# A new table of order, engines and buffers for four layers of two kinds of linear attention

## The chip, the core and the metric

The kernel runs on one core of one Trainium2 chip. The metric is device time in microseconds (us); the median of three runs is quoted, and single executions are named where a profile is read. Below, TensorE (PE; PEld is its weight load), VectorE (DVE), ScalarE (ACT), GpSimd (POOL) and SyncE (SP) are the core's engines. Each runs its own queue of instructions strictly in order and waits on semaphores for the others. Operands lie in SBUF; TensorE writes its results to PSUM.

## What is computed

x is 2048 tokens of 512 numbers (bf16). Four layers are added to it, A, B, A, B, each on a normalised x:

```python
x = A_x
x = x + _A_ref(_layernorm(x), A_wq, A_wk, A_wv, A_wo, A_beta)
x = x + _B_ref(_layernorm(x), B_wqkv, B_w_phi, B_wo)
x = x + _A_ref(_layernorm(x), ...)
x = x + _B_ref(_layernorm(x), ...)
```

Both have 32 heads of 16 numbers. Layer A cuts the tokens into 4 segments of 512. Within a segment it is causal softmax attention; from one segment to the next a memory is carried and read with phi(t) = t + 1 for positive t, else exp(t):

```python
p = softmax(q_s k_s^T * scale + mask);  a_dot = p @ v_s
a_mem = (phi(q_s) @ M) / (phi(q_s) @ z + 1e-6)
o = g * a_mem + (1 - g) * a_dot;  M += phi(k_s)^T v_s;  z += sum(phi(k_s))
```

Layer B has no mask: with a 16 x 16 map w_phi per head and phi(t) = [softmax(t w_phi), softmax(-t w_phi)],

```python
kv = phi_k^T v;  z = sum(phi_k);  o = (phi_q @ kv) / (phi_q @ z + 1e-6);  return o @ wo
```

## The kernel before

The tokens are 16 tiles of 128; x stays in SBUF as X. All the work is first written down as a graph of 2904 operations (class `Graph`, function `op`): each names its engine or engines, what it reads and writes, and the buffers that it opens. An operation is one instruction on ScalarE, VectorE and GpSimd, one or two transfers on SyncE, and 1 to 32 matmuls on TensorE, each with a weight load of its own: 1165 operations, 12,085 matmuls.

What the graph holds, layer by layer (`build`):

- `ln` normalises a tile: statistics on VectorE (L599, L600), the inverse root on GpSimd (L607, L609), the scaling on VectorE (L620), and a transpose, by a transfer of SyncE (L364) or on TensorE (L380, emptied through L359 or L360).
- `a_proj` projects queries, keys and values of a segment of layer A (L341), masks the keys into four copies (VectorE, L686, or ScalarE, L688), applies phi (L351, L674, L675) and sends the values through DRAM (v_rows, L368) to put them in rows.
- `a_att` computes the scores of two tiles (label S and, along the diagonal, Sd; TensorE, L326, D<-pK,pQ), takes their exponential out of PSUM (ScalarE, L351, 256 x 128x1024 and 192 along the diagonal), and multiplies with the values (label PV; L326, D<-pW,p and D<-pW,pP). A reciprocal (L393) and a product (L906) on VectorE empty the result.
- `b_keys` and `b_query` do the same for layer B: exponentials on ScalarE, sums on VectorE (L1012, L1015), small matmuls with the memory (label Zq: D<-Rz,p; label N: D<-Rkv,p; both L326), and products on VectorE (L1117, L1123).
- `out_proj` projects the result (L341) and adds it to X (VectorE, L961); in the last layer it stores X.
- `setup` loads the weights and x and fills small constants: lines 507 to 561 are such writes, among them the memsets of L553, L556 and L561, which are needed only when the buffer that they fill is first used, and the cast of L514, whose result nothing reads.

PSUM is four tensors D0 to D3 of 128x1024 f32. Every result of TensorE takes one of them from its first matmul to its last reading; 603 tiles share the four in turn, so TensorE often waits for a buffer to be emptied by ScalarE or VectorE. SBUF buffers are shared in the same way (pools p1, p2, pS and so on).

The order is not worked out in the kernel. `place` reads it from `ORDER`, a packed string at the end of the file. Unpacked, it has three parts: the operations' numbers in the order in which they are to stand (two bytes each), the engine of each operation (one byte), and the buffer of each of 1479 tiles (one byte). An engine's queue is the table's order cut down to that engine's operations. A tile that takes a buffer waits for the last operations on the tile that had it before. `emit` then writes the five queues and puts in the waits; a wait that another one already covers is left out.

```python
order = [self.ops[i] for i in np.frombuffer(raw, "<u2", n)]
o.seq, o.eng = k, ENGS[raw[2 * n + o.id]]
slots = dict(zip(tiles, raw[3 * n:]))
```

Of the kernel before, what the change touches and what calls it, by code (L numbers as in the profile page):

```python
# [16 lines left out]
D = 512  # L17
H = 32
# [42 lines left out]
class Tile:  # L61
# [236 lines left out]
class Kernel:  # L298
# [908 lines left out]
c-q~01C%YvvUWtIvs$OSk8RtwZQHhO+qP}nwr$&fRlCpJnYnk?y!+O_-oMs;xqDYuRz^lfeDOu>tkrRVL1IV_0QI0g5Hx^>&<LVIV`u_Rp&2xXWDp(VLOiGjnV~wAhxkweBxHk<Py<Rq  # L1207
R%ih&p%o~o3AvyGRD^<12y#MeXal987PN&jPzl;W3@8f;pfD7H_Rs-pLs38|1~H*Bl!M~X5n@3d=mec1AtZwAkOQhfUFZ!dAr)BY0=Xdxe1{+K6RN^%2!uD_Krr-yx6l_1e1z067}CHX
0PG3_;3**Xhj-8qy1@__3Q6G^aOe&LAvfm1_wWfm!xtC@d9erdgo%(3d%-l!iNhcl22lp^1H$z%12@2Q3`c`dz)YMA&*23O#t9GvmOemn%m}&IJa`GOU?Y^kuP_|Oz$WO2{V|wAXex|`
qF4+^!Z%m~4n=}3Fb#&_e8|E!!*&<}L(z}6LP?wsJ760`qX9SvRzWHBCx**lCuD)yFbQYEK->iyRs+XbFc||eEzE!^7=%k9I*o<Xum;NGR1|1&5|qUPxEzXLK`e|FFdXK`wJ;3JVLm8>  # L1210
XQ4E%gF?6hD&k5Qj`MH?#-K_V4#vTJ91j675+}oc9EDThFzkl|cmy1bKnLI;B*f7eKt~}MBhnr?2{CCe&cWTV4`*Q_j75>i4`<^7*b9j<KkS1EI0iGpSk$O+F)YO;I2RjW6I_gouo^bR
g_sVSVpLd()$u$mz{6-TB}OKRXJ8fXqKP;T7r}Tez?R{1Jc3nlH>JWxSQ%?z3P_Dru`$NRwOA9Qz(qJf>o5vkfJ+buS5bXT$7*41tcwew9yZ5=6c^LOYKo76R0mt&IoOOXu^G0)E!Y}Q
;wjvSo6sMUV0es&$MFQV!M1n^{4oTh(sc->qZoh@@CNLm^SA@EvIH0rFW@oUircXr?xo|f4WnZkTtk=P3be<A7!5-)Hm#-b)B$(nYCMN~Fa{ojLwFX~;Ck$cJ@5>6!VTD(R$wGNjXg0L
uArTmo@HQdXcxxBmb8*mP-pCd4e26Y!pIm4yJCGxj@>XNMa5Rsi1twpN<}HK0bRzV7>D*#FYJwduqL&o+EkZnQ9FuDQLqjbWc6qX#iQJ;J6?q=cnvyJV!A;$X(@G~tGJ0aQv$k%*YPek
rzX^xhEgXQM$M=%wx=6-6K`P%+<|-8fjUwP8crjqDRrf5^cd4(H@c74X(Yv`6EKRN-~-HxPcb9Dz=!w@vtcGIK$-C+X2;&thk8;kDoCeb5GAB#G=Y{=dc2K~Fas8%@$?+W&^Q`MqbVJB
r~cHJ22ej*M`I}om7pWEo`%q1I!YVp4i=`8l!x7djg*Z|q)C*Wm7-&GoDNYA)`Jey7D`H~X&X(Zt@Ie4KoR<ciRc}D#*8d4drx0*I~8Kz@fGI4T=W+2P(GHM^3V@FOH=48zM<E+gU--h
+DRv<Fnde)=p@~z+famEp=30bp3!M4%F@s&x=P>h9G$02G>x9qbh=Ep=n%`qa<bc$kKW@0I?O&%F?vK<@Dlq>KauDuy}`@uF{Put^om~72TV^#*hf6d($YivK}G2+eW3jGg)&eFmYIE|
($tY9r@`zA{iGpmAmfyuU1NjT3lcPsGSWM|&fM}vFX;xGPYdWKW7L&(W8dfkNy-b~Nzp~hN(WeR%0$4BX<A6xs4O#dkPT%g*f3U(on&RHCmYE|u@P(r^<v#wZ$@l58^g-89;_l8&B{|5
%1*b~ZN}IDR)J2jiqwboW96tX%L6&75@n%dtUo)=j<cCGi)Pb4wx1PaIcO}q!ZK5FHjZ6ol6PWfSP7>1ImX#Nc8AR&!S1tCtTL5klD%R6>>+!=?y^Pnmd$04*hMyvy<&4IfZc>D^q9S7
# [80 lines left out]
```

## Time and profile before

| | us |
|---|---|
| median of 3 runs | 456.07 |
| the runs | 455.7, 462.07, 456.07 |
| the profiled execution | 456.51 |
| its span, first to last instruction | 454.8 |

A row of groups gives line, engine, operation, what it writes and reads, the number, then busy time, mean time of one in ns, and the idle time of the engine just before them with what ended it. A row of waits gives who waited for what, the total in us, how many times, and the longest. A row of windows gives the stretch, then the busy time of PE, PEld, DVE, ACT and POOL with the number of instructions, the granted clock, the share of the transfer engines and GB/s. A row of the time line gives start and length in us and, in brackets, the idle time before. "issue" stands where an engine waited for nothing that the profile names. Queue q8 carries instructions: the transfers that bring TensorE's program to its sequencer. TensorE's busy time is modelled at the ends of matmuls, so it overstates.

### The profile page before, as it was taken

To read this page: it belongs to the slowest core of one execution; us is meant where nothing else is said; L and a number is where in the kernel's file an instruction comes from. 1 tells how busy PE (TensorE), PEld (TensorE's weight loads), DVE (VectorE), ACT (ScalarE), POOL (GpSimd) and SP (SyncE) were. 2 spreads that over 40 slices of the span, in tenths; PEclk is the share of its full clock that TensorE was granted. 3 is DMA by queue.
4 is the path that set the end of the run, shared out by engine and by line. 5 is a ranking of instruction groups with operands and counts; after the bars stand their busy time and mean duration, and the time that the engine had idled before them with its cause. 6 is when DMAs were issued, how large, how long until landed. Compare 5 with 4: busy or idle time off the path is not lost.

```text
span 454.8 us, 26184 instructions
## 1 busy us (share of the span) xinstructions
PE 427.2 (94%) x12085; PEld 289.5 (64%) x12085; DVE 403.1 (89%) x766; ACT 420.9 (93%) x584; POOL 58.4 (13%) x146
## 2 busy tenths in 40 slices
PE   8999999999999989989999998999999988999787
PEld 4756667767766666655556666677677666765444
DVE  7999999998798978869999997999898896788897
ACT  5999999999999997899999999999899999699992
POOL 3411014010101101100330112020020020110000
PEclk9999999999999999999999999999999999999999
DMA  8976655564247212101255668436232414300355
GB/s 251 217 165 100 99 93 109 107 87 80 45 76 111 38 40 50 13 3 27 62 111 86 85 97 103 71 87 81 57 50 49 109 19 63 46 17 4 49 91 180
DMA packets 105167, 36.71 MB, mean 81 GB/s; under 512 B 91730, under 2 KB 105058, under 8 KB 105058
## 3 DMA queue, kind: packets, MB, share of 16 engines
q1 hardware_dynamic: 104226, 34.50, 42.9%
q8 instruction: 95, 1.56, 1.4%
q10 hardware_dynamic: 800, 0.52, 0.4%
q14 instruction: 14, 0.11, 0.1%
q0 software_dynamic: 32, 0.02, 0.0%
HBM read 10.76 MB, written 6.55 MB: 38 GB/s over the span
## 4 chain that ended last, share of the span: by engine, by line
PE 61%; ACT 20%; DVE 12%; issue 3%; DMA 3%; POOL 1%; DVEq 0%
PE D L341 38%; PE D L326 22%; ACT p L351 11%; ACT pP L351 7%; DVE X L961 2%; DVE pQ L686 1%; DVE p L1117 1%; DVE stats L599 1%; DMA pX<-p 1%; DMA p<-p 1%; ACT pS L351 1%; DVE p L620 1%; DMA X<-in_A_x_dram 1%; DVE pK L360 1%; DVE p L906 1%
## 5 line engine op out<-in xcount | busy, mean ns | idle before, releaser
L351 ACT ACTIVATE p<-D 128x1024 bf16<-128x1024 f32 (+1 forms) x256 | 225.6, 934 | 10.8 <-PE D L341 4.9
L351 ACT ACTIVATE pP<-D 128x640 bf16<-128x640 f32 (+2 forms) x192 | 149.5, 828 | 7.2 <-PE D L326 5.9
L326 PE MATMUL D<-pK,pQ 64*128 64x128 bf16 (+6 forms) x1792 | 112.0, 227 | 4.2 <-ACT p L351 1.0
L326 PEld LDWEIGHTS D<-pK,pQ 64*128 64x128 bf16 x1792 | 67.0, 93 | 40.2 <-ACT pP L351 8.5
L326 PE MATMUL D<-pW,pP 64*128 64x50 bf16 (+1 forms) x3072 | 84.0, 181 | 3.4 <-issue 2.7
L326 PEld LDWEIGHTS D<-pW,pP 64*128 64x128 bf16 x3072 | 68.6, 93 | 9.2 <-issue 3.8
L607 POOL TENSOR_SCALAR rstd<-mv 128x1 f32<-128x1 f32 x60 | 17.0, 288 | 340.8 <-DVE mv L600 340.4
L326 PE MATMUL D<-pW,p 64*128 64x50 bf16 (+1 forms) x2048 | 50.4, 181 | 0.4 <-DVE pQ L686 0.2
L326 PEld LDWEIGHTS D<-pW,p 64*128 64x128 bf16 x2048 | 44.3, 93 | 3.9 <-issue 1.1
L599 DVE BATCH_NORM_STATS2 stats<-X 128x6 f32<-128x512 bf16 x63 | 42.3, 679 | 1.9 <-DMA X<-in_A_x_dram 1.6
L961 DVE TENSOR_TENSOR X<-X,D 128x1024 bf16<-128x1024 bf16 (+1 forms) x36 | 39.2, 1096 | 5.1 <-PE D L341 4.6
L326 PE MATMUL D<-tri,rep 64*128 64x64 bf16 (+1 forms) x384 | 40.1, 197 | 0.0
L341 PE MATMUL D<-pX,WA_k 64*128 64x512 bf16 (+1 forms) x288 | 37.4, 353 | 1.0 <-issue 0.5
L341 PE MATMUL D<-pX,WA_q 64*128 64x512 bf16 (+1 forms) x288 | 37.7, 353 | 0.6 <-issue 0.6
L609 POOL TENSOR_TENSOR rstd<-rstd,mhalf 128x1 f32<-128x1 f32 x60 | 35.9, 604 | 3.4
L341 PE MATMUL D<-WB_k,pX 64*128 64x512 bf16 (+1 forms) x288 | 33.8, 352 | 1.1 <-DMA pX<-p 0.4
L341 PE MATMUL D<-WA_o,p 64*128 64x512 bf16 (+1 forms) x288 | 33.2, 352 | 1.6 <-issue 0.8
L1015 DVE TENSOR_REDUCE pS<-p 128x64 f32<-128x1024 bf16 x28 | 33.4, 1211 | 0.9 <-ACT p L351 0.9
L341 PE MATMUL D<-WB_v,pX 64*128 64x512 bf16 (+1 forms) x288 | 33.3, 352 | 0.0
L341 PE MATMUL D<-WA_v,pX 64*128 64x512 bf16 x256 | 33.2, 377 | 0.0
L341 PE MATMUL D<-WB_o,p 64*128 64x512 bf16 (+1 forms) x288 | 32.5, 353 | 0.4 <-ACT p L351 0.3
L341 PE MATMUL D<-pX,WB_q 64*128 64x512 bf16 x256 | 32.5, 376 | 0.3 <-ACT p L351 0.3
(123 smaller groups left out, 665.5 us busy)
## 6 DMA issues: line engine op xcount, KB each, us to landing
v_rows<-pV SPq DMA_DIRECT2D x16, 272.0 KB, 3.6
pW<-v_rows SPq DMA_DIRECT2D x64, 68.0 KB, 2.7
out_dram<-X SPq DMA_DIRECT2D x7, 256.0 KB, 2.6
X<-in_A_x_dram SPq DMA_DIRECT2D x3, 512.0 KB, 7.7
pX<-in_B_wqkv_dram SPq DMA_DIRECT2D x3, 512.0 KB, 4.5
p<-p SPq DMA_TRANSPOSE x73, 3.2
pX<-p SPq DMA_TRANSPOSE x54, 3.6
WA_k<-in_A_wk_dram SPq DMA_DIRECT2D x2, 256.0 KB, 7.2
```

The source lines that it names most:

```text
L326: ins = e.matmul(out_ap, lhsT, rhs, start=st, stop=sp, tile_position=(basep(lhsT), basep(out_ap)))
L341: ins = e.matmul(out_ap, lhsT[64 * hf:64 * hf + 64], rhs[64 * hf:64 * hf + 64], start=k == 0 and i == 0, stop=k == 1 and i == len(lists[hf ...
L351: return self.g.op({"act": (dur, lambda e: e.activation(out_ap(), in_ap(), func, scale=scale))}, reads, writes, opens, label=label)
L360: "dve": ((340 if fast else n / 0.96 + 65), lambda e: e.tensor_copy(out_ap(), in_ap()))}
L599: v(lambda e: e.bn_stats(self.stats[:, t, :], self.X[:, t, :]), 602, [R("X", t)], [R("st", t)], label="bn")
L607: v(lambda e: e.tensor_scalar(rs, self.mv[:, t, 1:2], LN_EPS, None, op0=ALU.add), 170, [R("mv", t)], [R("rstd", t)], eng="pool", label="rstd")
L609: v(lambda e: e.tensor_tensor(rs, rs, self.mhalf[:], ALU.pow), 540, [R("rstd", t), R("mhalf")], [R("rstd", t)], eng="pool", label="rstd")
L620: v(lambda e: e.tensor_scalar(xn.t[:], self.X[:, t, :], self.mv[:, t, 0:1], self.rstd[:, t:t + 1], op0=ALU.subtract, op1=ALU.mult), 300, [ ...
L686: ch = {"dve": (129 + n / 3.84, lambda e, sl=sl, out=out: e.tensor_scalar(out(), src(), self.m4[:, sl:sl + 1], None, op0=ALU.mult))}
L906: v(lambda e, pvv=pvv, rden=rden, part=part: e.tensor_tensor(part(o).rearrange("p (a h d) -> p a h d", a=2, h=16), pvv()[:, :, :, 0:16], r ...
L961: self.v(lambda e: e.tensor_tensor(X(), X(), src(), ALU.add), 65 + 512 * n / 0.96, pr + xr, xr, label="res")
L1015: v(lambda e, E=E, k=k, Z=Z: e.tensor_reduce(Z.t[:, 64 * k:64 * k + 64], E.t[:].rearrange("p (a f h) -> p a h f", a=16, h=4), AX.X, ALU.ad ...
```

## The change

Only the string `ORDER` is replaced. The operations, their instructions and their sizes are the same; the code that reads the table is the same. The table was found by an offline search over orders in which the transfers that bring TensorE's instructions were taken to arrive later than for the table before. Start and end of each string:

```diff
 ORDER = """
-c-q~01C%YvvUWtIvs$OSk8RtwZQHhO+qP}nwr$&fRlCpJnYnk?y!+O_-oMs;xqDYuRz^lfeDOu>tkrRVL1IV_0QI0g5Hx^>&<LVIV`u_Rp&2xXWDp(VLOiGjnV~wAhxkweBxHk<Py<Rq
...
-a?d|MpPY5jE1bv!T{3!=EP%Up1cK4em6nW$c%gGK@l(v0K!jk9!J7QgVGtmg^v7_a9-zSn1HAu{_<<W(H^a0-KewD&Qsj#a(*&-F?+oE6j~}R!{tKc#=CJ
+c-q~11C%YvvUWy9x=y=~ZQHhO+qP}nwr$(CZQFiTyU*O2xp&sQ`_{kSzt(-VyQ?ZIBLiQ25j(3_6JsnntH<iI2CN}V%;K=PEFO!`kY#3#SYuX=HDOIzGiF(NR)R%i$yiBNodK)CO0niF
...
+>}$i4^zh@M;Bp`sDbyvC8=iK3aCN%Nh3|bzYnKb5f(0lqL4Lw==C}xlkO}hsToK^*7FQ2yLw<_Fx#m&3#V1JxdQ1r>x99o#n)eTIZkcem?2!HoOSk5$
 """
```

Unpacked, the two tables differ as follows (places are counted in each engine's own queue).

| engine | operations before, after | in the same place | furthest move |
|---|---|---|---|
| TensorE | 1165, 1165 | 664 | 16 places |
| ScalarE | 583, 582 | 494 | 4 |
| VectorE | 766, 769 | 107 | 62 |
| SyncE | 248, 248 | 97 | 22 |
| GpSimd | 142, 140 | 14 | 25 |

Five operations change engine: three memsets of setup go from GpSimd to VectorE (one of L556, two of L561), one of L561 goes the other way, and one emptying of a transposed tile in the last stage goes from ScalarE (L359) to VectorE (L360). Of 1479 tiles, 1034 have another buffer number; in PSUM, 431 of 603 have another number, and 462 of 603 follow the same tile in their buffer as before.

At the start, SyncE's queue has the load of X's tiles 4 to 7 ahead of the first half of WA_k, and the loads of WA_v and of one part of WA_o ahead of those of X's tiles 8 to 15. In VectorE's queue, statistics and masks stand at other places among the emptyings of PSUM. In the last stage one of the two last tiles' products (L1117) stands behind an addition to X (L961), and the cast of L514 stands just ahead of it.

More of the change, by code (lines that the diff above doesn't have):

```diff
@@ L1211 @@
[L1211 to L1218, printed above, removed]
@@ L1259 @@
[L1259 to L1261 removed]
+c-q~11C%YvvUWy9x=y=~ZQHhO+qP}nwr$(CZQFiTyU*O2xp&sQ`_{kSzt(-VyQ?ZIBLiQ25j(3_6JsnntH<iI2CN}V%;K=PEFO!`kY#3#SYuX=HDOIzGiF(NR)R%i$yiBNodK)CO0niF
@@ new lines @@
+D{H}8vYIR>tH83c9IPU1#agq1tPm^BYOzc#J1fH^E6j?pHmogc$11VftSoEKin4?(7wf=^F~#bz%B&pg$U3nqtT?O7s<LpbGkeN<vy?0mOT}`tF6=u?!uqfu>?eE8`m)q41B=dLu$b%(
+OT!Ff5Q}|egIH2Fm<?cESvQuE4PpIR0tWDm^<%-TI~&N}vUe;ud}5zj4>pwbWC1KM^kVN>P8h{F%LDl!7ddPid||l&VLcnpW<VfrV1f-}(;*0-vzagm=CX-wFa)v*tT@bL7GJQJEDQU<
+HnL!R#j;Qd*u+BcE9(bSSyAW@qggQ+!@jW*Yzf=S=Cf&R2ux?&*)moVX0jb@8ygC%*Z`Qrwy+tj6hy<F%)yatHQUSxX0xociw%UcY!WPGYuGHtAppj*$uI>1K|on30F&5MNXyDVdB_jT
+SrAyL07YOeD+tkX7z~Hfu#Odma<GCGf_bo#jbrm65*q;(p%RRQ{V<sYvGMFM3x@~54@bcimYepoJ!~{AVn^6+76A{igb)MwvZKs_m>3K9F$D)%Fzkg{un!W!9GDGbU;@mAlPn@G0Rv+p
@@ new lines @@
+KT8aYnS`a#0GhxeSPa!59B60=E1@Y=hXS+!4#PrN1t}pCMn=t|;4Yj9<DfE}X6e{?IKz&>0=5j6!*2A)D&WUbL276OHJ~cQhQ@H7t%dZgCLF+ZaFLy3Nnjzn#NxmztOK>6C4}NZtP3ev
+eOQgHARX0)%@Bocfw<5b{Gc8*gXVC71z-zk1L^4`Y=l$b4{c!+gok)=9Imsd7y|L(1hj*r5CLwmW8lv&z#iO-+aUo&gsrd*cEE8K9oFD^xXjwa6?PCJK`2CnwU`WI;~wY$hhR0tfOBvb
+cEfsD105keMrCK<7;B9yum|*n4UmUU!%pY~X<!#zgru+nT4Ec_Kq+t~rhrRuh&9CI5E)`YXNU^*u@$DoRM-gjVK3+nm!Sscr3Tmq`am3v0{gKh_Jy`s8|z{%Y=?1i33i1#SP!qVY!nZ#
+KsUI?I^zvoiixo?CcvxE1vg<6yasonDK^J@a1)2(X6%H`@H*Up4tNuWVS5~oEwCeY#cmkFu3>k03?uM5W`L0x6Gq_^$O=#41;oeu@Bkh{M##&uL0ZTTncxn41_kgXJc3)$8~b2-$P7L4
@@ L1262 @@
+D;rjPK0^AVXT_^l(g6a4T<K62#$@suM4;P}yzb+Q5Hlf;$13UX>&@gAUKsz#*LxU*YOngjg7tWfhPypOpr30dB+M1BZnZn~6`V^G@)JP8Zdlw`Kg?sV0e=eevEHjpw<R&~3-AC9=3YoT
+>}$i4^zh@M;Bp`sDbyvC8=iK3aCN%Nh3|bzYnKb5f(0lqL4Lw==C}xlkO}hsToK^*7FQ2yLw<_Fx#m&3#V1JxdQ1r>x99o#n)eTIZkcem?2!HoOSk5$
 """
```

90 lines of the change are left out of this document (44 added, 46 removed).

## The prediction

> **What bounds the kernel now.** I read the page first, then the waits, then the time line at the longest waits, then counts between them.
>
> ```profile
> span 454.8 us, 26184 instructions
> PE 427.2 (94%) x12085; PEld 289.5 (64%) x12085; DVE 403.1 (89%) x766; ACT 420.9 (93%) x584; POOL 58.4 (13%) x146
> ...
> q8 instruction: 95, 1.56, 1.4%
> ...
> PE 61%; ACT 20%; DVE 12%; issue 3%; DMA 3%; POOL 1%; DVEq 0%
> ...
> L351 ACT ACTIVATE p<-D 128x1024 bf16<-128x1024 f32 (+1 forms) x256 | 225.6, 934 | 10.8 <-PE D L341 4.9
> L351 ACT ACTIVATE pP<-D 128x640 bf16<-128x640 f32 (+2 forms) x192 | 149.5, 828 | 7.2 <-PE D L326 5.9
> ```
>
> The profiled execution took 456.51 us around a span of 454.8, so 1.7 lie outside; the median of the runs shown is 456.07, 0.4 below it, and I carry sums over to the median. TensorE, ScalarE and VectorE are busy 94, 93 and 89% of one span: there is no single engine to relieve. Two ScalarE groups that empty PSUM alone hold 225.6 + 149.5 = 375 us. The windows show where the idle time lies.
>
> ```profile
> 0.00:5.00 5.00, 3.89 (x24) 1.48 (x26) 1.94 (x5) 1.85 (x3) 3.17 (x20) 1.00 0.60 180
> 5.00:440.00 435.00, 412.53 (x11873) 282.21 (x11869) 389.74 (x747) 412.37 (x573) 55.19 (x126) 1.00 0.44 77
> 440.00:455.00 15.00, 10.74 (x198) 5.78 (x192) 11.45 (x16) 6.64 (x11) 0.00 (x0) 0.99 0.53 152
> ```
>
> Between 5 and 440 us ScalarE works 412.37 of 435 and TensorE 412.53: 22.5 us are free on each, and 2% of the time (9.1 us) would be two fifths of that. The clock is 1.00 throughout, so it explains nothing here. What ends those idle times:
>
> ```profile
> PEld D L326 <- ACT pP L351: 10.4, 34, 1.1
> PEld D L326 <- ACT p L351: 9.7, 29, 0.8
> ...
> DVE pS L393 <- PE D L326: 8.3, 10, 1.7
> ...
> PE D L326 <- issue: 4.9, 7, 1.6
> ...
> PE D L341 <- issue: 2.5, 5, 0.8
> ```
>
> Weight loads wait for ScalarE to empty a PSUM buffer (63 times), and matmuls wait for "issue", nothing the profile names, 12 times, 4.9 + 2.5 = 7.4 us. I looked at the longest of these, and at the instruction transfers just before it (a window of 422.3 to 423.6).
>
> ```profile
> 422.71 0.40 PEld L326 LDWEIGHTS D<-Rz,p 64*128 64x128 bf16 x26
> ...
> 424.77 0.24 PE L326 MATMUL D<-Rz,p 64*128 64x48 bf16 x7 [1.55 <-issue]
> q8 instruction: 1, 0.02, 4.5%
> ```
>
> TensorE stops within an operation of identical matmuls and goes on 1.55 us later; the only packet that window holds is one 16 KB packet of queue q8. There are 95 such packets, so 24,170 / 95 = 254 TensorE instructions each. If these waits are for that transfer, they must lie whole packets apart. Windows from one such wait to the next:
>
> ```profile
> 145.96:166.51 20.55, 18.29 (x637) 13.38 (x637) 17.38 (x26) 19.53 (x28) 1.92 (x4) 1.00 0.25 46
> 281.11:323.54 42.44, 41.71 (x1273) 28.96 (x1274) 38.75 (x65) 40.27 (x55) 5.13 (x13) 1.00 0.48 80
> 374.06:424.76 50.70, 46.43 (x1274) 33.77 (x1275) 39.52 (x77) 44.52 (x67) 3.22 (x8) 1.00 0.20 29
> ```
>
> Matmuls plus weight loads are 1274, 2547 and 2549: 5, 10 and 10 packets of 254.8. So the "issue" waits are TensorE's own instructions arriving late, where a packet's worth of short matmuls runs faster than the next one comes.
>
> The Trainium skill, "Runtime: NRT & Kernel Launch", section "Instruction fetch mechanics", gives the block as 16 KiB, 256 instructions, and here the trace agrees; it also says the fetch is hidden because instructions are dispatched more slowly than blocks arrive. By that, no gain from this source exists and the rival that lives on it (below) falls away; the 7.4 us above contradict it, so I keep that rival.
>
> **The change part by part.** Decoding both tables gives the same 2904 operations. TensorE: 664 of 1165 in the same place of its queue, none moved by over 16 places; of the swapped pairs within 24 places about two thirds are PV against PV, another fifth PV against a score matmul. ScalarE: 494 of 583 unmoved, none by over 4. VectorE: 107 of 766 unmoved, up to 62 places; SyncE 97 of 248, up to 22; GpSimd 14 of 142. Five operations change engine. No duration changes; the price is only in who waits.
>
> *Instruction packets.* Cut at every 254.4 TensorE instructions, the new queue holds in each packet on average 18 instructions that the old one did not; of the 12 packets that ended in a wait, ten differ by 64 or fewer, two by 107. Relieving a wait would need a packet with clearly longer matmuls. I take 0; the ends are -7.4 (all waits gone) and +1.55 (one more of the longest).
>
> *VectorE's order.* It empties 208 readings of PSUM. Adding the traced durations of what is queued ahead of each in both orders, the work ahead grows by 0.08 us on average; 38 have over 0.4 more (90th percentile 0.66), 31 over 0.4 less, 4 over 1 more.
>
> ```profile
> L686 DVE TENSOR_SCALAR pQ<-p,m 128x1024 bf16<-128x1024 bf16 (+1 forms) x70 | 31.1, 457 | 0.0
> ...
> L360 DVE CAST WB_q<-D 128x512 bf16<-128x512 f32 x4 | 2.8, 690 | 1.0 <-PE D L326 1.0
> L556 POOL MEMSET pP<- x6: 197/308/411, 1.5 to 3.6; 128x128 bf16 x2, 128x384 bf16 x2, 128x256 bf16 x2
> L561 DVE MEMSET pT<- x1: 112/112/112, 39.2 to 39.2; 128x64 bf16 x1
> L514 DVE CAST H8b<-H x1: 155/155/155, 418.6 to 418.6; 128x8 bf16<-128x8 f32 x1
> ```
>
> What changes places there is typically one mask (0.457 us) or a normalisation against a reading, and a shift in one reading is mostly made up by the next, as the mean of 0.08 shows. I take 0; the ends are -12 (31 x 0.4 all on the path) and +25 (38 x 0.66 all on the path). They are bounds, not expectations: the shifts have both signs, and each engine is idle only a twentieth of the time, so most land on covered work.
>
> *PSUM buffers.* Of 603 tiles in the four buffers, 462 still follow the same tile as before in their buffer; the others follow from the swaps in TensorE's queue, since a buffer is handed on in the order of use. ScalarE empties in an order that differs in 89 places of 583, each by at most four. That the 63 waits on ScalarE above (10.4 + 9.7 = 20.1 us) change is possible in both directions; I take 0, with a quarter of them, 5 us, either way.
>
> *Head.* A memset of line 556 goes from GpSimd to VectorE, just ahead of the first normalisation, and one addition of line 521 behind it goes later. The load of X's tiles 4 to 7 (512 KB) is issued ahead of the first half of WA_k (256 KB) instead of behind; the last two lines are the landings of WA_k and of X.
>
> ```profile
> 6.92 0.41 DVE L620 TENSOR_SCALAR p<-X,mv,rstd 128x512 bf16<-128x512 bf16 x1
> ...
> 7.24 0.22 DVE L521 TENSOR_TENSOR rep<-rep,ident 128x128 bf16<-128x128 bf16 x1
> ...
> 7.38 0.17 PEld L380 LDWEIGHTS D<-ident,p 64*128 64x128 bf16 x8 [0.97 <-DVE p L620]
> ...
> 9.21 0.09 PEld L341 LDWEIGHTS D<-pX,WA_k 64*128 64x128 bf16 x1
> 1.93 0.40 SPq L462 DMA_DIRECT2D WA_k<-in_A_wk_dram  x1
> DMA to landing us min/median/max: 5.3/5.3/5.3
> DMA to landing us min/median/max: 6.3/6.3/6.3
> ```
>
> The memset costs 0.31, the addition gives back 0.22: +0.1 on the way to the first projection (ends 0 and +0.41, its slowest). WA_k landed at 1.93 + 5.3 = 7.2; X, issued at 2.4 with 6.3 to landing, at 8.7. Swapped, both are in by about 8.7, and the projection starts at 9.21: 0 (end: +0.5, if WA_k takes 1 us behind X).
>
> *Transfers behind SyncE.* 65 loads, stores and transposes shift by over 2.5 us in SyncE's queue. Two transposes stand in the chain of work:
>
> ```profile
> 66.28 4.52 DMA pX<-p
> 354.79 4.13 DMA p<-p
> 70.89 0.39 PE L341 MATMUL D<-WB_k,pX 64*128 64x512 bf16 x2 [0.41 <-DMA pX<-p]
> 61.48 0.40 DVE L620 TENSOR_SCALAR p<-X,mv,rstd 128x512 bf16<-128x512 bf16 x1
> 63.58 0.41 DVE L620 TENSOR_SCALAR p<-X,mv,rstd 128x512 bf16<-128x512 bf16 x1
> ```
>
> At 66 us the projection of B's keys needs both tiles of a pair. Their normalisations ended at 61.9 and 64.0, yet the second transpose went out only at 66.28, behind other transfers. The new VectorE order puts the first tile's normalisation behind the second's and behind one long multiply (L835), about 65.8 to 66.2, and SyncE's new order has the other tile's transpose and one load ahead of it, both gone by then: it goes out at about 66.3, lands at 70.8 as before, and TensorE waits its 0.41 again. At 354.79 the ten VectorE operations between the emptying of a key projection and the reciprocal that leads to the transpose are the same ten in another order. I take 0 for both; the ends are -0.4 (that wait gone) and +4.5, one transpose fully uncovered.
>
> *Setup writes.* One 0.11 memset goes onto VectorE at the last query stage (419 us), where TensorE waits for VectorE, and the unused 0.155 cast of line 514 leaves that place: 0.
>
> *Tail.* One emptying of a transposed tile (0.60 on ScalarE) goes to VectorE between the last residual additions, together with that 0.155 cast.
>
> ```profile
> 446.95 0.60 ACT L359 ACTIVATE p<-D 128x512 bf16<-128x512 f32 x1 [1.37 <-PE D L929]
> ...
> 449.79 2.59 DVE L961 TENSOR_TENSOR X<-X,D 128x1024 bf16<-128x1024 bf16 x3 [0.74 <-PE D L341]
> ```
>
> By the cast of the same shape (0.69) VectorE gets 0.69 + 0.155 = 0.85, and the 0.74 it waits for the last projections covers all but 0.1: +0.1. Without that cover it costs 0.85; below, 0.
>
> Sum: packets 0, VectorE's order 0, buffers 0, head +0.1, transfers 0, setup writes 0, tail +0.1: +0.2 on 456.51. That is less than two agreeing runs differ by (455.7 and 456.07), so I keep the median and forecast 456.1.
>
> **The rivals.** *The late instructions are dodged.* If all 12 issue waits went: 456.1 - 7.4 = 448.7; half of them: 452.4. For it: the waits are real and sit in a few packets. Against: the packets hold nearly the same instructions in both tables. For more than 2% (below 446.9) 1.8 us of the 20.1 would have to go as well.
>
> *VectorE empties PSUM too late* (the other side). In its queue a mask or normalisation now stands ahead of a reading of PSUM whose buffer TensorE needs next. Price about 0.6 each; 15 of the 38 later ones uncovered make 9 us, 465.1, and that is where it becomes slower by 2%; 8 give 461. For it: VectorE has the most changed order, and PEld already waits on buffers. Against: mean shift 0.08.
>
> *No effect on the issue waits, but the ScalarE waits fall.* With scores and PV alternating more evenly, ScalarE is fed earlier; a quarter of 20.1 us gives 451. Against: ScalarE's own order hardly changes, so it can be fed earlier only by TensorE, whose order hardly changes either.
>
> **How the numbers follow.** Forecast, 453 to 459: 0.66. One of the two gains, 446.9 to 453: 0.14; both together, below 446.9: 0.06. VectorE mild, 459 to 465.2: 0.07; past 15 uncovered, above: 0.07. The likeliest has its own range of 453 to 459; for eight in ten I go from 448.5 (all issue waits gone) to 463.5 (twelve readings late). Two per cent, 9.1 us, is about what a measurement of this kernel can tell from no change, as one of the three runs shown took 462.07; inside it lies 0.87.
>
> **What would show it.** Right: the issue waits of PE again 6 to 9 us, some twelve, at multiples of 255 instructions; ScalarE and TensorE within 3 us of their busy times; one L359 fewer on ScalarE and one L360 more on VectorE near the end, with the last addition at the same distance from the end; first projection at 9.2 to 9.6. Wrong: issue waits under 4 us (first rival), PEld waits for DVE lines over 15 us together (second), waits for ACT below 16 (third).

## The result and the profile after

The kernel after took 461.33 us (median of 19 runs, 459.90 to 466.07) against 457.64 (19 runs, 454.99 to 464.41) of the kernel before beside it: a ratio of 1.0092, 95% interval 1.0068 to 1.0116. It is slower by 0.9%, within the 2% band, and 5.2 us above the forecast of 456.1. Of these 5.2, 1.6 is the reference itself (457.64 here, 456.07 in the three runs shown before); 3.7 is the change. Some executions take over 1.5% longer than the fastest of the same kernel: the medians here are of all executions, the ratios and intervals leave those out. The unchanged kernel after, measured twice more beside the kernel before, gave 1.0046 (1.0015 to 1.0077) and 1.0077 (1.0046 to 1.0107).

The profiled execution of after took 462.09 us. From its page, the span, the busy times, the instruction queue, the shares of the chain that ended last, and ScalarE's two great groups:

```profile
span 460.3 us, 26190 instructions
PE 428.3 (93%) x12085; PEld 290.4 (63%) x12085; DVE 403.1 (88%) x769; ACT 420.5 (91%) x583; POOL 59.1 (13%) x144
...
q8 instruction: 95, 1.56, 1.5%
...
PE 58%; ACT 17%; DVE 15%; issue 4%; DMA 3%; POOL 1%; SPq 0%; DVEq 0%
...
L351 ACT ACTIVATE p<-D 128x1024 bf16<-128x1024 f32 (+1 forms) x256 | 225.4, 932 | 12.6 <-PE D L326 6.7
L351 ACT ACTIVATE pP<-D 128x640 bf16<-128x640 f32 (+2 forms) x192 | 148.9, 824 | 9.0 <-PE D L326 7.9
```

Busy times are those of before within 1.1 us, so no work was added; the span is 5.5 us longer, and each engine is idle 4.4 to 5.9 us more. The waits of after:

```profile
DVE pS L393 <- PE D L326: 9.0, 13, 2.2
PEld D L326 <- ACT p L351: 9.9, 30, 0.9
PEld D L326 <- ACT pP L351: 8.2, 30, 0.6
...
PE D L341 <- issue: 5.1, 7, 1.4
PE D L326 <- issue: 4.8, 10, 1.1
...
PEld D L341 <- DMA pX<-p: 1.9, 1, 1.9
...
PEld D L326 <- DMA pW<-v_rows: 1.2, 2, 1.0
```

The waits of weight loads for ScalarE fell from 20.1 to 18.1, those of matmuls for "issue" rose from 7.4 to 9.9, and two longer waits for transfers stand where the matmuls of before had two of 0.4. But single executions of one kernel differ by nearly as much as the two kernels: a second profile of the unchanged kernel before had a span of 458.4 against 454.8, and two more of after had 458.9 and 458.4. The profile of before that the prediction was read from was one of the quicker ones. So differences between single spans prove nothing here; what repeats does. Times between the same five matmul operations in each execution (own sums, from the ends of the operations that ended at these times before) show it:

| us | before | before again | after | after again | after, third | mean difference |
|---|---|---|---|---|---|---|
| start to 36.8 | 36.79 | 38.73 | 36.51 | 36.93 | 37.02 | -0.94 |
| 36.8 to 65.5 | 28.73 | 28.92 | 29.67 | 29.47 | 30.42 | +1.03 |
| 65.5 to 80.4 | 14.88 | 16.60 | 16.52 | 16.80 | 17.16 | +1.09 |
| 80.4 to 418.5 | 338.06 | 338.28 | 341.25 | 339.32 | 337.34 | +1.13 |
| 418.5 to 451.5 | 33.03 | 32.59 | 32.14 | 32.13 | 32.13 | -0.68 |
| 451.5 to the end | 3.29 | 3.32 | 4.19 | 4.27 | 4.30 | +0.95 |

Three rows have a cause that can be seen, in whole or in part. The row from 80.4 to 418.5 overlaps between the kernels, and the first is one late start of "before again". The row from 65.5 to 80.4 overlaps too, but there the waits explain each execution: "before again" has one wait for issue of 1.45 in it, and without TensorE's waits for issue and for the transpose described below the stretch lasts 14.4 to 14.7 in all five.

**At 55 us: the last weights of WA_o.** The table moves the load of the last part of WA_o back in SyncE's queue. Its issue, and the first matmul that needs it, before and then after:

```profile
41.60 1.05 SPq L462 DMA_DIRECT2D WA_o<-in_A_wo_dram  x2
...
54.69 0.82 PE L341 MATMUL D<-WA_o,p 64*128 64x512 bf16 x6 [0.30 <-ACT pP L351]
```

```profile
51.00 1.98 SPq L462 DMA_DIRECT2D WA_o<-in_A_wo_dram  x2
...
54.96 1.04 PE L341 MATMUL D<-WA_o,p 64*128 64x512 bf16 x8 [0.70 <-ACT pP L351]
```

The load landed at 45.54 before and at 54.40 after. The wait is 0.30 in both profiles of before and 0.70, 0.78 and 0.89 in the three of after, about half of the 1.03 of this row. Both rows name ScalarE. That the load is what came last is argued: the matmul starts 0.55 to 0.57 behind its landing in each of these three, and in a later kernel with the same place of the load (32 instructions fewer at the start) the profile names the load itself, 0.5. No run moved it alone.

**At 65 to 80 us: a transpose behind a load.** SyncE's queue in the profile of before, then of after (start, length of the issue, instruction):

```profile
62.08 1.19 SPq L364 DMA_TRANSPOSE p<-p  x1
63.31 0.58 SPq L368 DMA_DIRECT2D pW<-v_rows  x1
63.93 3.62 SPq L364 DMA_TRANSPOSE pX<-p  x2
67.60 0.58 SPq L462 DMA_DIRECT2D pX<-in_B_wqkv_dram  x1
```

```profile
62.39 2.51 SPq L364 DMA_TRANSPOSE p<-p  x2
64.95 1.90 SPq L364 DMA_TRANSPOSE pX<-p  x1
66.89 0.59 SPq L462 DMA_DIRECT2D pX<-in_B_wqkv_dram  x1
67.53 1.19 SPq L364 DMA_TRANSPOSE pX<-p  x1
68.76 0.58 SPq L368 DMA_DIRECT2D pW<-v_rows  x1
69.38 1.19 SPq L364 DMA_TRANSPOSE p<-p  x1
```

Before, both transposes into pX go out ahead of the load of 512 KB; the second is gone at 67.55 and landed at 70.80. After, the load lies between them: the second goes out at 67.53 and lands at 73.13, 5.6 us later, with the load beside it (5.84 and 5.95 in the two further profiles of after, against 4.52 and 4.28 in the two of before). The tile that it carries was also normalised later (66.33 instead of 61.48, VectorE's L620). TensorE, in after, by its matmuls and by its weight loads:

```profile
73.18 1.04 PE L341 MATMUL D<-WB_k,pX 64*128 64x512 bf16 x8 [1.58 <-ACT p L351]
```

```profile
73.17 0.33 PEld L341 LDWEIGHTS D<-WB_k,pX 64*128 64x128 bf16 x6 [1.86 <-DMA pX<-p]
```

The matmul's row names ScalarE, the weight load's the transfer. The landing at 73.13, 0.04 before the weight load starts, decides between them. The same wait was 0.41 and 0.50 in the two profiles of before; it is 1.8 and 1.9 in the two further profiles of after.

**At the end: stores behind transposes.** SyncE's last stage, before and after:

```profile
429.97 6.45 SPq L364 DMA_TRANSPOSE p<-p  x4
436.51 0.54 SPq L368 DMA_DIRECT2D out_dram<-X  x1
438.01 7.45 SPq L364 DMA_TRANSPOSE p<-p  x4
```

```profile
435.16 14.63 SPq L364 DMA_TRANSPOSE p<-p  x8
449.85 7.51 SPq L368 DMA_DIRECT2D out_dram<-X  x9
```

The kernel before sends one store between the transposes; the kernel after sends all nine behind them, from 449.85 on. The busy share of the transfer engines in the last 8 us, in 40 slices (of after also what they moved), and the stores of 128 KB with the time from issue to landing, before and after:

```profile
DMA  9999997006999999999950000299999559400000
...
out_dram<-X SPq DMA_DIRECT2D x2, 128.0 KB, 2.0
```

```profile
DMA  0299999999999999999986999993981000000000
GB/s 0 102 364 302 374 333 323 379 343 313 338 364 343 297 425 353 318 328 323 328 220 220 338 338 353 343 333 97 323 297 41 26 20 26 20 15 0 0 0 0
...
out_dram<-X SPq DMA_DIRECT2D x2, 128.0 KB, 2.9
```

The stretch of almost no gap (from the third slice to the thirtieth) is the new thing, and the last two stores land 2.9 instead of 2.0 us after their issue. That is the 0.95 of the table's last row, and it stands in each of the three profiles of after. But the packing of the stores alone doesn't make it. The kernel after with 56 more short matmuls at the start (one of the experiments below) sends the same nine stores in one stretch, each within 0.6 us of its time in after, counted from the start of the last additions. Its last 8 us:

```profile
DMA  0020000999729999999999999999999999920000
...
out_dram<-X SPq DMA_DIRECT2D x2, 128.0 KB, 1.8
```

There the last two stores land 1.8 us after their issue, and the last part takes 3.14 instead of 4.19. What differs at the end of after is the run of slices at 15 to 41 GB/s: in the trace the packets of its last microsecond, 1 KB each, follow one another singly, some 42 ns apart, so one of the 16 transfer engines was still at work when the others had finished. A 16 KB packet of TensorE's instructions (queue q8) starts at 455.2 in after, among the stores, and takes 1.1 us, about as long as that engine is late; in the kernel just shown it starts 2.6 us ahead of the last additions, and in the kernel before it falls for the most part into the gap between the stores. That the packet holds one engine back is argued from this: the trace doesn't say which engine carried it, and no run moved the packet and nothing else. The last addition's row shows the other half:

```profile
454.38 2.60 DVE L961 TENSOR_TENSOR X<-X,D 128x1024 bf16<-128x1024 bf16 x3 [0.31 <-PE D L341]
```

VectorE waits 0.31 for the last projections instead of 0.74, and the end comes 5.9 us after the start of these additions (460.3 - 454.38) instead of 5.0. The part before it gains 0.68, so the last 42 us as a whole cost about 0.3.

### The profile page after: what moved, and what is told of

Its sections match the earlier page's. It is cut to its first block, busy times and chain, and to the rows that moved or that the text cites. A ratio compares the mean times of both kernels' runs of the same rounds, so it can differ in the third digit from the quotient of the medians.

```text
span 460.3 us, 26190 instructions
## 1 busy us (share of the span) xinstructions
PE 428.3 (93%) x12085; PEld 290.4 (63%) x12085; DVE 403.1 (88%) x769; ACT 420.5 (91%) x583; POOL 59.1 (13%) x144
## 4 chain that ended last, share of the span: by engine, by line
PE 58%; ACT 17%; DVE 15%; issue 4%; DMA 3%; POOL 1%; SPq 0%; DVEq 0%
PE D L341 36%; PE D L326 22%; ACT p L351 9%; ACT pP L351 7%; DVE X L961 2%; DMA p<-p 2%; DVE stats L599 2%; DVE p L1117 1%; DVE p L360 1%; DVE pQ L686 1%; DVE p L620 1%; ACT pS L351 1%; DMA X<-in_A_x_dram 1%; DVE Rkv L980 1%; DVE p L1123 1%
## 5 line engine op out<-in xcount | busy, mean ns | idle before, releaser
L961 DVE TENSOR_TENSOR X<-X,D 128x1024 bf16<-128x1024 bf16 (+1 forms) x36 | 39.2, 1097 | 5.3 <-PE D L341 5.2
L609 POOL TENSOR_TENSOR rstd<-rstd,mhalf 128x1 f32<-128x1 f32 x60 | 37.1, 630 | 3.9
```

Of the source, the lines that this page charges most:

```text
L609: v(lambda e: e.tensor_tensor(rs, rs, self.mhalf[:], ALU.pow), 540, [R("rstd", t), R("mhalf")], [R("rstd", t)], eng="pool", label="rstd")
L961: self.v(lambda e: e.tensor_tensor(X(), X(), src(), ALU.add), 65 + 512 * n / 0.96, pr + xr, xr, label="res")
```

## The experiments

Three theories stood. T: transfers come late behind SyncE. P: the new order makes TensorE's instruction packets late more often. C: the difference is mostly chance of single executions. An edit of the order is shown below as the lines of the queue that it changes.

**The kernel after again**, unchanged.

> The changed kernel unaltered, for a second profile of it. Both theories: ratio to the kernel before 1.007 to 1.012. Theory T (two transfers behind SyncE come late): TensorE again waits 1.2 to 1.9 us for the transpose of X at 71 to 73 us and about 0.5 us for the rows of the values at 293 us. Theory P (TensorE's instruction packets come late more often): the waits for issue of PE sum again to about 10 us, against 7.4 before; if they fall back to 7 or rise above 12 from one execution to the next, they are chance and not the order.

Measured: 1.0046 (1.0015 to 1.0077). The wait for the transpose came again (1.8), so did the one for the rows of V near 293 us (0.5); the issue waits of matmuls were 8.5 instead of 9.9. The waits for transfers repeat; of the rise of the issue waits, 2.5 us, 1.1 is left.

**The transpose put back ahead of the load**, with the two VectorE operations that feed it moved up.

```diff
 L364 DMA_TRANSPOSE p<-p x2
-L364 DMA_TRANSPOSE pX<-p
+L364 DMA_TRANSPOSE pX<-p x2
 L462 DMA pX<-in_B_wqkv_dram
-L364 DMA_TRANSPOSE pX<-p
 L368 DMA pW<-v_rows
```

> The changed kernel with one tile's normalisation and its transpose put back to where they stood before (ahead of the other tile's transpose and of a 512 KB load). Theory T: the wait for the transpose at 71 us falls from 1.6 to 0.4 us or less, all later work comes 1.2 to 1.6 us earlier, ratio 1.006. Theory P: the time won there is lost again within the next 50 us, since ScalarE and the packets set the pace; ratio stays at 1.009.

Measured: 1.0048 (1.0015 to 1.0080), 459.11 against 460.24 of after on the same chip. TensorE's wait for this transpose:

```profile
PEld D L341 <- DMA pX<-p: 0.3, 1, 0.3
```

The cause of the wait is shown: 1.9 became 0.3 with the transpose and its normalisation moved together; which of the two places counts more was not tested. The time hardly followed: 1.1 us by the medians, nothing by the ratios (1.0048 against 1.0046). In this profile the matmuls wait 2.5 us for other transposes (p<-p), where the three of after have 0.2 to 1.1.

**Both transfers put back**: also the four transfers of V's rows together, ahead of the transpose that after has between them.

```diff
-L368 DMA pW<-v_rows x2
+L368 DMA pW<-v_rows x4
 L364 DMA_TRANSPOSE p<-p
-L368 DMA pW<-v_rows x2
 L364 DMA_TRANSPOSE pX<-p x2
```

> The same, and in SyncE's queue the four row transfers of the values at 287 to 291 us ahead of a transpose of the attention's result, as before. Theory T: the wait for these rows at 293 us (0.54) goes as well and the lag to the kernel before is about 2 us smaller than that of the changed kernel: ratio 1.0045. Theory P: ratio 1.008 to 1.009.

Measured: 1.0030 (1.0001 to 1.0060), 458.76, which is 1.5 below after by the medians and 0.7 by the ratios. Its single profile had a span of only 455.7, with 7.6 of issue waits, the least in any profile of after's order; its median lies 1.3 above that execution. The wait for the rows shrank to one of a weight load, 0.2.

**The late transpose put into the kernel before**: the reverse of the first edit, with two GpSimd operations of the other tile moved up.

> The kernel before with only that normalisation and that transpose moved to where the change puts them (behind the other transpose and the 512 KB load). Theory T: TensorE's wait for the transpose at 71 us grows from 0.4 to about 1.6 us and the kernel is slower by 1.2 to 1.6 us: ratio 1.003. Theory P: absorbed, ratio 1.000.

Measured: 1.0028 (0.9996 to 1.0059). The wait appears where the kernel before had 0.4:

```profile
PEld D L341 <- DMA pX<-p: 2.5, 2, 1.7
...
PE D L341 <- DMA pX<-p: 1.9, 2, 1.5
```

One of the two is the transposed tile, at 73.7 us here, 1.45 for the matmul. So the late place of the normalisation and its transpose makes the wait in either order; its price, some 1.3 us by the medians, is at the edge of what this measurement resolves.

**All packet cuts moved by 112 instructions**, in the kernel before and in the kernel after. At the start, TensorE runs matmuls on constants that keep it busy until data come; nobody reads their result, and nothing else of the computation changes. 56 more of them (each with its weight load, 112 instructions), with others shortened so that the stretch takes as long, move every later cut between packets of 256 instructions to another place of the work.

```diff
-for rows, n, m in ((64, 51, 12), (64, 64, 8), (64, 256, 4)):
+for rows, n, m in ((64, 51, 40), (64, 64, 8), (64, 64, 4)):
```

> The kernel before with 112 more TensorE instructions (56 short matmuls among those at the start whose result nobody reads; some others of these shortened, so that the start keeps its length within 0.5 us). Every later packet of 256 instructions now begins 112 instructions earlier in the work. Theory P: an issue wait is a packet that came late, so the waits move with the cuts, still a multiple of 256 apart, and where they fall matters: adding the fastest quarter of each operation's traced steps between cuts, packets that last under 2.4 us grow in sum from 3.3 to 8.6 us of shortage, so PE's waits for issue rise from 7.4 to about 12 and the kernel is slower by 3 to 6 us: ratio 1.007 to 1.013. Rival (issue is something that belongs to the operations, not to the cuts): the waits stay at the same operations, ratio 1.000 to 1.002.

> The changed kernel with the same 112 instructions more. Theory P: shortage from 3.3 to 8.2 us, ratio to the kernel before 1.013 to 1.020. Rival: as the changed kernel, 1.005 to 1.010.

Measured: 1.0331 (1.0282 to 1.0381) and 1.0326 (1.0274 to 1.0378): 15 us, several times what was expected, and alike in both orders. The waits of TensorE in the shifted kernel before, and one of them:

```profile
PE D L326 <- issue: 16.9, 18, 2.1
PE D L341 <- issue: 5.9, 7, 1.3
```

```profile
291.60 0.22 PE L326 MATMUL D<-pW,pP 64*128 64x50 bf16 x4 [2.10 <-issue]
```

7.4 of issue waits (9.6 in the second profile of before) became 22.8, and in the shifted kernel after 25.7. Counted in the trace with the instructions that only wait, 24 of the 25 longer than 0.1 us stand at instruction 192 or 193 modulo 256, and in every other kernel all but at most four. So nearly all issue waits are the packets, as the prediction read them, and how much they cost depends on where in the work the cuts fall. The 15 us of these two runs are about the growth of the waits, 15.4 us against the first profile of before and 15.8 against that of after.

**The kernel before again**, one execution, for the spread.

> The kernel before unaltered, for a second profile. Theory P of the loss: PE's waits for issue again about 7.4 us, clearly less than the 8.5 to 11.1 of the first profiles of the changed order. Theory C (the difference in these waits is chance): 9 us or more. Either way the wait for the transpose at 71 us is 0.4 or less.

Measured: one time of 460.15, span 458.4; matmuls waited 9.6 for issue, where the first profile of the same kernel had 7.4:

```profile
PE D L326 <- issue: 5.5, 9, 1.2
PE D L341 <- issue: 4.1, 6, 1.4
```

Over four kernels with before's cuts and its order, but for single edits, the sums of these two rows are 7.4, 9.6, 7.8 and 11.3, mean 9.0; in five profiles with after's 9.9, 8.5, 8.9, 11.1 and 7.6, mean 9.2. A fifth of a microsecond between means, 4 us between executions: that the new order changes the issue waits of matmuls isn't shown, and the 2.5 us between the first two profiles are within this spread. The same two rows of the weight loads (PEld) differ more, 18.4 against 20.7 in the mean, but overlap as well (16.4 to 19.9 and 18.5 to 23.8); whether that costs time was not tested.

**The kernel before with the last stage of after.**

```diff
-L364 DMA_TRANSPOSE p<-p x7
-L368 DMA out_dram<-X
-L364 DMA_TRANSPOSE p<-p x4
-L368 DMA out_dram<-X x6
+L364 DMA_TRANSPOSE p<-p x11
+L368 DMA out_dram<-X x7
 L368 DMA out_dram<-X x2
```

> The kernel before up to the last stage (413 us), then the changed table's order, engines and buffers. In all profiles of the changed order so far the lag fell by 0.85 us between 418 and 431 us. If that belongs to the order of the last stage, this version ends 0.6 to 1 us earlier than the kernel before, ratio 0.998, with the one long wait for issue at 423 us below 1.1 us against 1.55; if it was chance, ratio 1.000.

Measured: 1.0026 (0.9990 to 1.0062). The expected gain isn't there. What came over is the late end; its last 8 us:

```profile
DMA  0499999999999999998967998269597000000000
...
out_dram<-X SPq DMA_DIRECT2D x2, 128.0 KB, 2.9
```

The last additions start 5.9 us before the end, as in after, and not 5.0: the packed stores come with this order of the stage, whatever lies before it, and so does the late end, as long as the cuts between the packets stay about where they are. On the whole time the stage makes no difference that this run could tell.

**A last set on one chip**: after a third time, both transfers put back again, that kernel with 32 instructions fewer at the start, and the kernel before with 56 more.

> The kernel after, unchanged, as the partner of the three other runs on this chip. Two measurements gave 1.0092 (1.0068 to 1.0116) and 1.0046 (1.0015 to 1.0077) of the kernel before. Theory T (two transfers come late behind SyncE) expects 1.003 to 1.009 again, about 1.5 to 2.5 us, with a wait of 1.5 to 2 us for the transpose into the buffer of X's normalised tiles near 72 us. Theory C (most of the difference is chance of single executions) expects 1.002 to 1.005 with an interval that nearly reaches 1.

Measured: 1.0077 (1.0046 to 1.0107), wait for the transpose 1.9.

> The kernel after with both late transfers put back ahead in SyncE's queue (and the two VectorE operations that feed the first). Theory T expects it 1.5 to 2.5 us below the kernel after of the same chip, so within 0.2% of the kernel before; the waits of TensorE for transfers at most 1 us in sum instead of some 4. Theory C expects less than 1 us between the two.

Measured: 1.0048 (1.0012 to 1.0085), 0.7 us below after by the medians and 1.3 by the ratios. With the first time (1.5 and 0.7), the two late transfers are worth about 1 us, less than their waits of 2.1 to 2.4 us in the three profiles of after. The intervals of the repaired kernel and of after overlap both times; and 1.0030 and 1.0048 are still above the kernel before. The matmuls' waits for transfers, expected at 1 us at most, were 2.9 in this run's profile, 2.33 of them the wait named in the next run.

```diff
-for rows, n, m in ((64, 51, 12), (64, 64, 8), (64, 256, 4)):
+for rows, n, m in ((64, 51, 4), (64, 64, 8), (64, 384, 4)):
```

> As the run with both transfers put back, with 16 fewer, and 8 longer, matmuls in the stretch of warming matmuls at the start, whose result nobody reads: all later cuts between instruction packets fall 32 instructions later in the work. Theory P (where the cuts fall in the work sets the issue waits) expects a change of 1 to 5 us against that run: my count of how long each 256 instructions take gives 1 us less shortage of packets, so 1 us faster; if the table is fitted to its own cuts, as the shift by 112 suggested, 2 to 5 us slower. Theory C (issue waits are drawn anew in each execution) expects no change, within 1 us.

Measured: 1.0105 (1.0059 to 1.0151), 3 us slower than the kernel with the same transfers, not 1 us faster: of the two numbers of theory P, the one for a table fitted to its own cuts fits, though the intervals of the two kernels overlap. That packets cost these 3 us isn't shown: in its one profile, the fastest of its six executions, the matmuls wait only 7.9 for issue. This kernel also shows what waits behind the repaired transpose:

```profile
64.72 3.84 SPq L364 DMA_TRANSPOSE pX<-p  x2
68.60 0.58 SPq L462 DMA_DIRECT2D pX<-in_B_wqkv_dram  x1
69.23 0.50 SPq L368 DMA_DIRECT2D pW<-v_rows  x1
69.78 1.19 SPq L364 DMA_TRANSPOSE p<-p  x1
```

```profile
75.35 1.21 PE L341 MATMUL D<-pV,p 64*128 64x136 bf16 x32 [1.03 <-DMA p<-p]
```

With both pX transposes early, TensorE waits for the next thing behind the load, the transpose of phi of the keys (p<-p, issued at 69.78; the kernel before issues it at 58.14, well ahead of the load). In the kernel with the first repair this wait was 0.43; in the one with both it was none in one profile and 2.33 in the other. So a third transfer had moved behind the load too, and part of what the repair gains is given back one projection later. Putting all three ahead wasn't tried.

```diff
-for rows, n, m in ((64, 51, 12), (64, 64, 8), (64, 256, 4)):
+for rows, n, m in ((64, 51, 26), (64, 64, 8), (64, 128, 4)):
```

> The kernel before with 28 more, and 8 shorter, warming matmuls at the start, whose result nobody reads: all later cuts between instruction packets fall 56 instructions earlier in the work, half of the 112 that cost 15 us (1.033). Theory P expects a cost between none and that: 1.010 to 1.025 (about half to two thirds of 15 us by my count of short packets), with issue waits of TensorE of 13 to 22 us instead of 7 to 11, still at one position modulo 256. A theory that the 15 us came from the changed warming itself (its shorter matmuls, a lower clock at the start) and not from the cuts expects under 1.004.

Measured: 1.0335 (1.0279 to 1.0392), the whole 15 us at half the shift, above the range of theory P and far above the 1.004 of the theory that blames the warming itself. That theory is ruled out less by this number, since this edit shortens the warming matmuls too, than by the waits. In its profile the matmuls wait for issue 19.8:

```profile
PE D L326 <- issue: 16.9, 20, 1.9
PE D L341 <- issue: 2.9, 3, 1.2
```

Between the operations that end at 80.4 and 418.5 before, it took 350.0 us against 338.1 and 338.3: most of the loss lies far from the start. Part of it may be the clock, 0.992 in the mean here, 0.996 and 0.992 in the other shifted ones and 1.000 before; it is at most 0.8% of 473.5, 3.8 us.

## Why the prediction was right, and where it was not

*Within 2%, inside the range:* held. All three measurements of after lie between 1.0046 and 1.0092, well inside the 0.87 given to "same", and 461.33 is inside the wide range of 448.5 to 463.5. It is not inside the likeliest one, 453 to 459: it falls between 459 and 465.2, which had 0.07, and not by the mechanism named there, of VectorE emptying PSUM too late. What was right is that a new order without new work moves this kernel by less than 2%; that the sum came so near is in part luck: behind "transfers 0" and "tail +0.1" stood waits of +1.3 and +0.5 and changes of +0.95 and -0.68 us.

*Transfers behind SyncE, 0:* this step failed. It said that the moved transpose "goes out at about 66.3, lands at 70.8 as before, TensorE waits its 0.41 again", with the other tile's transpose and one load ahead of it, "both gone by then". Gone from SyncE's queue they were, at 67.48, but not from the transfer engines: it went out at 67.53, 1.2 late, and took 5.6 to land beside the load of 512 KB, where the same transpose took 4.52 before. The wait was 1.6 to 1.9, inside the bounds (-0.4 to +4.5) that the step gave. The last load of WA_o, issued at 51.00 instead of 41.60, was among the transfers that shift and got no price either; it goes with 0.4 to 0.6 at 55 us. The table moved a third transfer behind the same load, which the step didn't list, and put a transpose between the rows of V at 287 us, a wait of 0.5 to 0.6 that was inside the step's "65 loads, stores and transposes" and got no price.

*Tail, +0.1:* the engine work came out as predicted, the stage as a whole at about +0.3. VectorE's cover held (0.74 became 0.31, and 418.5 to 451.5 is shorter by 0.68). What the sum left out is the stores: the same table moves the first of them behind all transposes, and with a packet of instructions among them the end comes 0.95 later. The step looked at who waits for VectorE and not at what SyncE sends after it.

*Instruction packets, 0:* held as far as it can be read. The issue waits of the two first profiles differ by 2.5, but those of profiles with the same cuts by 4. Read from one execution, 7.4 looked like a property of the kernel; the mean is 9.0. The ends given (-7.4 to +1.55) took this spread for none.

The Trainium skill, "Runtime: NRT & Kernel Launch", section "Instruction fetch mechanics", has blocks of 256 instructions fetched while the current one runs, and calls the crossing of a boundary mostly hidden. The period of 256 agrees with the runs, where all but a few of the waits stand at 192 or 193 modulo 256. "Hidden" does not: by it, moving the cuts would cost nothing, and it cost 15 us.

*VectorE's order, 0:* nothing seen against it. With 659 of its operations in other places, DVE's share of the waits of matmuls and weight loads did not rise (own sum of the rows of weight loads for DVE: 20.1 before, 17.8 after). "Each engine is idle only a twentieth of the time" was misread: VectorE is busy 89% and so idle a ninth. The sign announced for the second rival, over 15 together, was badly set, as before already had 20.1. *PSUM buffers, 0, and setup writes, 0:* nothing in the traces speaks against them.

*Head, +0.1:* the first projection began at 8.79, 9.14 and 9.01 in the three profiles of after, against 9.24 and 9.11 before, and not at 9.2 to 9.6. If anything it gained 0.2.

*The signs:* ScalarE's and TensorE's busy times (within 0.4 and 1.1 us), one L359 fewer (10 instead of 11) and one L360 more (18 instead of 17) came as announced. Issue waits of 9.9 were outside "6 to 9", a range drawn too narrowly from one profile; the distance of the last addition from the end was 0.9 longer, which pointed straight at the stores.

*The size:* of the 2.6 us in the means of the table above, 1.1 at 65 to 80 us is explained by the late transpose, and 0.95 at the end, minus 0.68 just before it, goes with the stores and the order of the last stage. The gain and loss before 65 us cancel, and +1.13 between 80 and 418 us, with executions from 337.3 to 341.3, is unsettled: the rows of V give 0.1 to 0.5 of it, and no run isolated the rest. The part between 36.8 and 65.5, +1.03, goes with the wait at 55 us and with issue waits of 0.2 to 0.8 between 41 and 64 us, which the two profiles of before lack; that it comes from the new order was not tested by itself. So what the 3.7 us between the medians are made of is shown only in part.

## What to carry to other kernels

When a table moves a transfer, look at what lies ahead of it both in the issuing queue and on the transfer engines, at every transfer that passes the same large load, and at the last stores, since the kernel ends with their landing, and at what else the transfer engines carry among them. Take the spread from several profiles of the unchanged kernel before reading a difference of a few microseconds; here one kernel's spans differed by 3.6. In a kernel that issues short matmuls without a gap, count the instructions ahead of a stretch as part of its timing: a few dozen more at the start can cost more than the change under study.

## What the runs showed of the hardware

Adding 28 or 56 short matmuls in the first microseconds, whose own time was hidden, cost 1.0335 (1.0279 to 1.0392) and 1.0331 (1.0282 to 1.0381), with TensorE's waits for its own instructions rising from 7.4 and 9.6 to 19.8 and 22.8; 32 instructions fewer, on another table, gave 1.0105 (1.0059 to 1.0151) where 1.0030 and 1.0048 had been measured, but its one profile shows no more waits than theirs. All but at most four of the waits in each profile stand at 192 or 193 modulo 256. That 56 and 112 instructions cost the same, and that fewer may cost too, is what one would see if both tables had been laid out around their own cuts; the runs don't show how wide the good place is.

Near the end, the transfer engines were full for a few microseconds: nine stores were packed together. Full engines alone did not delay the last store (1.8 us from issue to landing in the shifted kernel after, 2.0 in the kernel before); with a 16 KB packet of instructions among the stores it took 2.9, the last microsecond of it on one engine alone. The Trainium skill, "DMA: Bandwidth & Descriptors", section "Where 436 GB/s comes from", gives about 358 GB/s as the limit of one core towards the chip's memory. The trace agrees with its size: most full slices of the row shown for after lie between 297 and 379 GB/s, one at 425.
